# Reciprocals on a second engine, a paired fifth tile and a new order in a fused attention and feed-forward kernel

## The chip, the cores and the metric

The kernel runs on one core of one Trainium2 chip. A core has TensorE (matrix products; its weight loads are listed apart as PEld), VectorE (DVE), ScalarE (ACT), GpSimd (POOL) and SyncE (SP, which issues DMAs here). Each engine works through its own instructions in order; semaphores tie them together. The metric is device time in microseconds (us), the median of several runs. One more run was taken with the hardware profiler; its first to last instruction is called the span.

## The reference

Eight batches of eight heads, sequence 576, head size 64. Per head a linear attention with a cosine weighting, then a feed-forward layer with the activation h cos h over all 4608 tokens:

```
def phi(x, c, s):
    r = np.maximum(x, 0.0)
    return np.concatenate([r * c, r * s], axis=-1)
q_p = phi(q, cos_w, sin_w);  k_p = phi(k, cos_w, sin_w)
kv = einsum('bhsf,bhsd->bhfd', k_p, v);  z = sum(k_p, axis=2)
num = einsum('bhsf,bhfd->bhsd', q_p, kv)
den = einsum('bhsf,bhf->bhs', q_p, z)[..., None] + 1e-06
x = num / den            # (b, s) rows, 8 * 64 = 512 columns
h = x @ w_in             # 512 -> 2048
out = (h * cos(h)) @ w_out   # 2048 -> 512
```

## The kernel before

**Tiles.** A batch has 576 tokens: four tiles of 128 and a rest of 64, the fifth tile. Raw q, k and v lie in `raw[nm]`, 128 partitions by eight heads by five tile places. Batches of even and odd number use opposite halves: batch b writes five places of every second partition (`go5` in `load`, L332) and four places of the others (`go4`), so the fifth place of a batch fills only 64 partitions, and the other 64 keep what was there. Two batches' rests make one full tile of tokens: the feed-forward part runs over nine chunks of 512 tokens, eight from the full tiles of the batches and the ninth (`xR`) from the four paired fifth tiles.

**Attention.** `prep` (L355) applies relu and the cosine or sine weight (a column of `CS` per tile) to one tile, on ACT or VectorE, and writes 16-bit values to `KQ`. `cast_v` (L369) makes V 16-bit, with a column of ones, so that `kv` (L383) gives the product and the sum z in one. A tile of q is transposed by TensorE (`q_pe`, L414, batches 0 and 1) or by a transposing DMA on SP's queue (`q_dma`, L426). `num` (L435) multiplies it with `kvz`, takes the denominators (`den`, L468 and L470, eight per partition), their reciprocal (L474, VectorE) and the normalized tile (`x16`, L476, VectorE), in this order; the reciprocal and the normalization are one step of the plan, `norm`. `x_pe` or `x_dma` transposes the result to `xT`.

The fifth tile of q is scaled, transposed and kept per batch, in `qT4[0]` and `qT4[1]`. Both full-width products are added up in the PSUM bank, each batch with zero rows at the other's place; that is why the fifth place of q is set to zero at the start (L962). `late_q0` (L1039) does this for batch 0 during the first layer 1.

**Feed-forward.** `layer1` (L522) multiplies with `w_in`; `gate` (L511) takes the cosine on ACT and the product on VectorE; `layer2` (L813) multiplies with `w_out`. From chunk 3 on parts of both use a scheme with seven instead of eight products, with sums on VectorE (`sums`, L321).

**Order.** The code adds steps to a `Plan` (L142). `KEYS` (L17) holds a number for each step, found beforehand: its place in the overall order, and in the last digit which of the allowed engines takes it (`pick`, L186). `run` sorts by these places and issues; nothing is decided on the chip. Every engine gets its instructions in that order, DMAs included: loads and stores on SP, the weights' loads on POOL. Some small POOL casts (`hold_raw`, L945, and the `hold` functions in L920 to L958) write one element of a buffer only to make a following load wait until the time is right.

Of the kernel before, what the change touches and what calls it, by code (L numbers as in the profile page):

```python
# [11 lines left out]
ALU = mybir.AluOpType  # L12
F32 = mybir.dt.float32
# [180 lines left out]
def kernel(  # L194
# [9 lines left out]
    nc = tc.nc  # L204
    B, H, S, D = q.shape
    Dm, Dff = moe_w_in.shape
    P = 128
# [886 lines left out]
```

## Time and profile before

| what | value |
|---|---|
| runs | 280.79 us median of 3 (280.42 to 281.32) |
| the profiled execution | 280.85 us, span 279.0 us |
| busy | TensorE 269.2, VectorE 251.4, ACT 218.9, GpSimd 8.3 us |
| reciprocals (L474) | 36, 197 ns each |
| normalizations (L476) | 32 of 512 columns at 692 ns, 8 half ones at 421 and 414 ns |
| transposing DMAs of q (L428) | 30 |
| first matmul of layer 1 | 20.44 us from the span's start |

How to read it: the groups of a profile page name line, engine, operation, what is written from what, shape and count, then the busy time and the mean duration of one in ns, then the idle time of the engine just before them and what ended it. In the timeline the first column is the start in us, the second the duration. A releaser is written behind an arrow. The time of the run is larger than the span by what lies around it (1.85 us here).

### The profile page before, as it was taken

The numbers are of one execution on the slowest core, as the hardware profiler recorded it, in microseconds if no ns is written. First come the engines' busy times: TensorE is split into PE (matmuls) and PEld (weight loads), VectorE is DVE, ScalarE is ACT, GpSimd is POOL, SyncE is SP. The second block draws the span as 40 slices with busy tenths as digits, with TensorE's granted clock in tenths as the row PEclk, the third lists the DMA queues.
The fourth block names the chain that finished last, engine by engine and source line by source line (L and its number), as shares of the span: only waits on it lengthen the run. The fifth ranks groups of instructions, "written<-read, shape, count | busy, mean of one in ns | idle before, by whom it ended". The sixth has DMA issues, their size and how long they took to land.

```text
span 279.0 us, 6853 instructions
## 1 busy us (share of the span) xinstructions
PE 269.2 (96%) x2715; PEld 217.3 (78%) x2715; DVE 251.4 (90%) x449; ACT 218.9 (78%) x401; POOL 8.3 (3%) x21
## 2 busy tenths in 40 slices
PE   7779999999999999999999999999999999999994
PEld 2458767678766677789879887998788888888883
DVE  2977798999999999999999999999999999998872
ACT  2856698899999999999999999984684686777210
POOL 1430020000000000000000000000000000000000
PEclk9999999999999999999999999999999999999999
DMA  6999999999999999999999999737210400200324
GB/s 208 315 201 232 281 312 282 309 218 172 328 269 253 210 288 247 310 235 230 245 264 195 346 277 265 154 58 205 39 39 4 188 2 0 78 0 2 151 78 150
DMA packets 77599, 53.30 MB, mean 191 GB/s; under 512 B 46080, under 2 KB 75264, under 8 KB 77568
## 3 DMA queue, kind: packets, MB, share of 16 engines
q1 hardware_dynamic: 72608, 48.12, 67.7%
q0 software_dynamic: 4224, 4.19, 9.3%
q10 hardware_dynamic: 736, 0.57, 0.6%
q8 instruction: 21, 0.34, 0.5%
q14 instruction: 10, 0.08, 0.1%
HBM read 36.74 MB, written 9.44 MB: 166 GB/s over the span
## 4 chain that ended last, share of the span: by engine, by line
PE 85%; DMA 5%; ACT 4%; DVE 3%; issue 2%; ACTq 0%
PE M L849 33%; PE M L685 15%; PE M L542 8%; PE M L582 7%; PE TR L685 6%; PE M L784 4%; PE ATT L450 3%; DMA qT<-KQ 3%; PE ATT L391 3%; DMA qm<-in_q_dram 2%; ACT KQ L364 2%; PE TR L582 1%; ACT ch L514 1%; PE M L420 1%; DVE KQ L365 1%
## 5 line engine op out<-in xcount | busy, mean ns | idle before, releaser
L514 ACT ACTIVATE ch<-M 128x512 f32<-128x512 f32 x90 | 53.9, 603 | 14.0 <-PE M L685 6.8
L849 PEld LDWEIGHTS <-gT 128*128 128x128 f16 x560 | 54.1, 98 | 8.2
L519 DVE TENSOR_TENSOR gT<-M,ch 128x512 f16<-128x512 f32 x84 | 55.9, 685 | 4.5 <-ACT ch L514 4.0
L849 PE MATMUL M<-w_out_sb,gT 128*128 128x256 f16 x448 | 56.4, 273 | 0.0
L364 ACT ACTIVATE KQ<-km,CS 128x512 f16<-128x512 f32 x56 | 38.9, 732 | 0.5 <-DMA km<-in_k_dram 0.5
L364 ACT ACTIVATE KQ<-qm,CS 128x512 f16<-128x512 f32 x48 | 33.5, 728 | 4.4 <-DMA qm<-in_q_dram 4.2
L685 PEld LDWEIGHTS <-w_in_sb 128*128 128x128 f16 x320 | 31.0, 98 | 4.6 <-issue 0.2
L849 PE MATMUL M<-T,S 128*128 128x256 f16 x256 | 31.5, 273 | 0.0
L318 ACT ACTIVATE ost<-M 128x512 f32<-128x512 f32 x32 | 19.2, 600 | 15.0 <-PE M L849 9.5
L542 PE MATMUL M<-xT,w_in_sb 128*128 128x256 f16 x256 | 30.1, 272 | 0.6 <-DVE gT L519 0.5
L542 PEld LDWEIGHTS <-w_in_sb 128*128 128x128 f16 x256 | 24.6, 98 | 4.8 <-issue 1.2
L582 PE MATMUL M<-xT,w_in_sb 128*128 128x512 f16 x112 | 27.9, 379 | 0.0
L849 PEld LDWEIGHTS <-S 128*128 128x128 f16 x256 | 24.9, 98 | 3.4
L476 DVE TENSOR_TENSOR x<-ATT,rec 128x512 f16<-128x512 f32 x32 | 22.1, 692 | 2.5
L685 PEld LDWEIGHTS <-WS 128*128 128x128 f16 x216 | 20.6, 98 | 2.6
L582 PEld LDWEIGHTS <-w_in_sb 128*128 128x128 f16 x128 | 11.9, 98 | 9.2
L365 DVE TENSOR_SCALAR KQ<-qm,CS 128x512 f16<-128x512 f32 x32 | 14.2, 479 | 4.8 <-DMA qm<-in_q_dram 4.8
L450 PEld LDWEIGHTS <-qT 128*128 128x128 f16 x320 | 14.7, 98 | 4.4 <-issue 1.4
L323 DVE TENSOR_TENSOR S<-gT 128x2048 f16<-128x2048 f16 (+1 forms) x16 | 17.2, 1083 | 0.0
L450 PE MATMUL ATT<-kvz,qT 128*128 128x65 f16 x288 | 15.3, 194 | 0.9 <-DVE kvz L406 0.4
L323 DVE TENSOR_TENSOR gT<-Z,ch 128x1024 f16<-128x1024 f32 x13 | 15.9, 1219 | 0.3
L698 DVE TENSOR_TENSOR Z<-M,Z 128x512 f32<-128x512 f32 x22 | 14.9, 686 | 0.9 <-PE M L685 0.5
(138 smaller groups left out, 448.6 us busy)
## 6 DMA issues: line engine op xcount, KB each, us to landing
out_dram<-ost SPq DMA_DIRECT2D x33, 256.0 KB, 2.7
qm<-in_q_dram SPq DMA_DIRECT2D x8, 640.0 KB, 5.7
km<-in_k_dram SPq DMA_DIRECT2D x8, 640.0 KB, 6.5
qm<-in_q_dram SPq DMA_DIRECT2D x8, 512.0 KB, 6.0
km<-in_k_dram SPq DMA_DIRECT2D x8, 512.0 KB, 6.5
vm<-in_v_dram SPq DMA_DIRECT2D x6, 640.0 KB, 6.8
vm<-in_v_dram SPq DMA_DIRECT2D x6, 512.0 KB, 6.6
w_in_sb<-in_moe_w_in_dram POOLq DMA_DIRECT2D x4, 512.0 KB, 8.6
```

The source lines that it names most:

```text
L318: "ACT": lambda: nc.scalar.activation(out=out_, in_=in_, func=AF.Copy),
L323: return lambda: q.tensor_tensor(out=out_, in0=in0, in1=in1, op=op)
L364: fn = {"ACT": lambda: nc.scalar.activation(out=out_, in_=in_, func=AF.Relu, scale=sc), "DVE": lambda: nc.vector.tensor_scalar(out=out_, i ...
L365: "DVE": lambda: nc.vector.tensor_scalar(out=out_, in0=in_, scalar1=0.0, scalar2=sc, op0=ALU.max, op1=ALU.mult)}
L450: nc.tensor.matmul(bank[hb][:, hh * D1:(hh + 1) * D1], lhsT=a[:, h, :], rhs=z[:, h, :], start=(i == 0), stop=(i == len(parts) - 1))
L476: nc.vector.tensor_tensor(out=split(x16[n][:, hs, :], k), in0=A[:, :, :, 0:D], in1=split(rec[n][:, hs], k).unsqueeze(3).broadcast_to((P, k ...
L514: act(0.5, due, lambda: nc.scalar.activation(out=ch[c], in_=bank, func=AF.Sin, bias=math.pi / 2.0, scale=1.0), [key], [("ch", c)])
L519: dve(0.61, due, lambda: nc.vector.tensor_tensor(out=dst, in0=a, in1=b, op=ALU.mult), [key, ("ch", c), *rd], dkeys)
L542: nc.tensor.matmul(M1[m][:, jj * 2 * P:(jj + 1) * 2 * P], lhsT=w_in_sb[:, cc, j * P:(j + 1) * P], rhs=X[:, cc, ts], start=(jj == 0 and cc ...
L582: nc.tensor.matmul(M, lhsT=w_in_sb[:, cc, j * P:(j + 1) * P], rhs=X[:, cc, :], start=(cc == 0), stop=(cc == NCT - 1))
L685: nc.tensor.matmul(bank[0][:, j * TH:(j + 1) * TH], lhsT=a(cc, j), rhs=b[:, cc, :], start=(first and j == 0 and cc == 0), stop=(last and j ...
L849: nc.tensor.matmul(bank[0][:, tt * MH:(tt + 1) * MH], lhsT=a[:, j, tt * P:(tt + 1) * P], rhs=b[:, j, :], start=(first and (apart or tt == ...
```

## The change

1. The reciprocal becomes a step of its own. On VectorE it is the same instruction; on GpSimd it is a power: `den` to the power of `NEG8`, a new tile of eight values of minus one. 23 of the 36 go to GpSimd, two of them in the first attention (tiles 0 and 2 of batch 0) and 21 in batches 2 to 7.
2. The fifth tile of q is scaled and transposed once per pair of batches, at the odd one, over all 128 partitions; a new column of `CS` holds its weights for both. There is one `qT4`. Its product takes 64 columns of `qT4` (every second) for each batch and writes them to 64 neighbouring partitions, so the rows of that tile are in another order, which the last stores undo. `late_q0` and the zeroing of q go.
3. All places in `KEYS` are new, and so is the choice of engine for some steps: of q's and k's scalings, V's casts (two of batch 1 go to GpSimd) and copies from PSUM. In the first attention, the load of the third quarter of `w_in` now stands behind the first power on POOL.

```diff
-    cs_np = np.zeros((P, 2, 2, NT + 1), dtype=np.float32)
+    cs_np = np.zeros((P, 2, 2, NT + 2), dtype=np.float32)
...
+            cs_np[n::2, :, g, NT + 1] = w[NT:S5:NT + 1, None]
...
+    NEG8 = sb("NEG8", [P, 8], F32)
...
-    qT4 = [sb(f"qT4_{n}", [P, H, P]) for n in range(2)]
+    qT4 = sb("qT4", [P, H, P])
...
-        sc = CS[:, b % 2, g, t:t + 1]
+        sc = CS[:, b % 2, g, t + (nm == "q" and t == NT):][:, 0:1]
...
-                for i, (a, z) in enumerate(parts):
+                for n2 in range(2) if t == NT else [None]:
+                    rows_, cols, z = (slice(0, P), slice(0, P), kvz[b % 2]) if n2 is None else (
+                        slice(n2 * R, (n2 + 1) * R), slice(n2, P, 2), kvz[n2])
                     nc.tensor.matmul(
-                        bank[hb][:, hh * D1:(hh + 1) * D1], lhsT=a[:, h, :], rhs=z[:, h, :],
-                        start=(i == 0), stop=(i == len(parts) - 1))
+                        bank[hb][rows_, hh * D1:(hh + 1) * D1], lhsT=a[:, h, cols], rhs=z[:, h, :],
+                        start=True, stop=True)
...
+        either(due, {"DVE": 0.14, "POOL": 0.3}, {
+            "DVE": lambda: nc.vector.reciprocal(out=rec[n], in_=den[n]),
+            "POOL": lambda: nc.gpsimd.tensor_tensor(out=rec[n], in0=den[n], in1=NEG8, op=ALU.pow)},
+            [("den", n, h) for h in range(H)], [("rec", n)], port=False, hint=2)
+
         def norm():
-            nc.vector.reciprocal(out=rec[n], in_=den[n])
             for A, (hs, k, ks) in zip(N, cut):
...
-            put(due, dst.rearrange("i (p t) m -> p t i m", t=NT + 1)[:, NT], blocks(O, n)[:, i0:, f],
+            put(due, dst.rearrange("i (p t) m -> p t i m", t=NT + 1)[:, NT], O[n * R:(n + 1) * R, i0:, f],
...
-        for i, nm in enumerate("qkv"):
+        for i, nm in enumerate("kv"):
             dve(0.53, i - 9, lambda nm=nm: nc.vector.memset(raw[nm][:, :, NT, :], 0.0), [],
...
-        for t in range(NT + 1):
+        for t in range(NT + b % 2):
...
-    late_q0()
```

More of the change, by code (lines that the diff above doesn't have):

```diff
@@ L226 @@
             w = fn(theta)
-            cs_np[n::2, n, g, :] = w[:S5].reshape(R, NT + 1)
+            cs_np[n::2, n, g, :NT + 1] = w[:S5].reshape(R, NT + 1)
+            cs_np[n::2, :, g, NT + 1] = w[NT:S5:NT + 1, None]
             cs_np[1 - n::2, n, g, :NT] = w[S5:].reshape(R, NT)
@@ L237, in sb @@
         return pool.tile(shape, dt, name=name)
-    CS = sb("CS", [P, 2, 2, NT + 1], F32)
+    NEG8 = sb("NEG8", [P, 8], F32)
+    CS = sb("CS", [P, 2, 2, NT + 2], F32)
     IDENT = sb("IDENT", [P, P])
@@ L411, in qdst @@
     def qdst(b, t):
-        return (qT[t], ("qT", t)) if t < NT else (qT4[b % 2], ("qT4", b % 2))
+        return (qT[t], ("qT", t)) if t < NT else (qT4, "qT4")
     def q_pe(b, t, bank, key, eng, due):
@@ L439, in num @@
         keys = [p[1] for p in pair] if pair else [("ATT", 0), ("ATT", 1)]
-        parts = [(qdst(b, t)[0], kvz[b % 2])]
+        a = qdst(b, t)[0]
         rd = [qdst(b, t)[1]] + [("kvz", b % 2, i) for i in range(2)]
         if t == NT:
-            parts.insert(0, (qT4[1 - b % 2], kvz[1 - b % 2]))
-            rd += [("qT4", 1 - b % 2)] + [("kvz", 1 - b % 2, i) for i in range(2)]
+            rd += [("kvz", 1 - b % 2, i) for i in range(2)]
         def mm(hb):
@@ L448, in mm @@
                 h = hb * HB + hh
-                for i, (a, z) in enumerate(parts):
+                for n2 in range(2) if t == NT else [None]:
+                    rows_, cols, z = (slice(0, P), slice(0, P), kvz[b % 2]) if n2 is None else (
+                        slice(n2 * R, (n2 + 1) * R), slice(n2, P, 2), kvz[n2])
                     nc.tensor.matmul(
-                        bank[hb][:, hh * D1:(hh + 1) * D1], lhsT=a[:, h, :], rhs=z[:, h, :],
-                        start=(i == 0), stop=(i == len(parts) - 1))
+                        bank[hb][rows_, hh * D1:(hh + 1) * D1], lhsT=a[:, h, cols], rhs=z[:, h, :],
+                        start=True, stop=True)
         full.update((key, False) for key in keys)
         for hb in range(2):
-            pe(HB * len(parts), MMA, due, lambda hb=hb: mm(hb), rd, [keys[hb]])
+            pe(HB * (1 + (t == NT)), MMA, due, lambda hb=hb: mm(hb), rd, [keys[hb]])
         if pair is None:
@@ L479, in norm @@
                     op=ALU.mult)
-        dve(0.9 if pair is None else 1.02, due, norm, keys + [("den", n, h) for h in range(H)], [("x16", n)])
+        dve(0.7 if pair is None else 0.82, due, norm, keys + [("rec", n)], [("x16", n)])
         return n
@@ L767, in store_tile @@
             dst = out.rearrange("(i n s) m -> n i s m", n=2, s=S)[n][2 + i, 0:S5, 0:MH]
-            put(due, dst.rearrange("(p t) m -> p t m", t=NT + 1)[:, NT], blocks(ost[o], n)[:, i, 0:MH],
+            put(due, dst.rearrange("(p t) m -> p t m", t=NT + 1)[:, NT], ost[o][n * R:(n + 1) * R, i, 0:MH],
                 [("ost", o, 0, i)], *((nc.scalar, "ACT") if n else (nc.sync, "SP")), nb=65.5)
@@ L908, in setup @@
         nc.gpsimd.memset(V1[:, :, :, D], 1.0)
+        nc.gpsimd.memset(NEG8, -1.0)
     wi = moe_w_in.rearrange("(c p) f -> p c f", p=P)
@@ L1037, in attention @@
                 x_dma(b, t, n, due + 1)
-    def late_q0():
-        for g in range(2):
-            prep(0, "q", NT, g, "DVE", 24, after=[("g", 0, 0, 0)])
-        q_pe(0, NT, TR, ("TR", 0), "ACT", 25)
     first_attention()
     layer1(0)
-    late_q0()
     second_attention()
```

244 rows, old and new, of the table KEYS are left out of this document.

## The prediction

> **What bounds the kernel now.** I read the page's busy times and its chain that ended last, then the busy times by stage.
>
> ```profile
> PE 269.2 (96%) x2715; PEld 217.3 (78%) x2715; DVE 251.4 (90%) x449; ACT 218.9 (78%) x401; POOL 8.3 (3%) x21
> PE 85%; DMA 5%; ACT 4%; DVE 3%; issue 2%; ACTq 0%
> ```
> ```profile
> 20.00:40.00 20.00, 19.34 (x164) 15.04 (x162) 16.24 (x32) 14.84 (x26) 1.66 (x3) 1.00 1.15 277
> 40.00:80.00 40.00, 39.90 (x449) 29.86 (x448) 38.14 (x83) 37.20 (x76) 0.00 (x0) 1.00 1.05 267
> 80.00:134.00 54.00, 53.56 (x585) 42.40 (x583) 51.97 (x91) 52.90 (x102) 0.00 (x0) 1.00 1.11 247
> 134.00:188.00 54.00, 53.93 (x581) 45.28 (x580) 52.61 (x92) 52.19 (x95) 0.00 (x0) 1.00 1.01 228
> 188.00:242.00 54.00, 54.00 (x497) 46.80 (x495) 52.46 (x83) 34.95 (x61) 0.00 (x0) 1.00 0.23 70
> ```
> The columns are stretch, length, then PE, PEld, DVE, ACT and POOL busy. TensorE is the bound from 20 us on, at full clock. A busy matmul may still wait, so I also compared the distance of neighbouring matmul starts in the trace with their usual pace (109 ns for 256 columns, 216 for 512, 30 for 65, 56 for a transpose). What exceeds the pace adds up to 3.35 us after 20 us: 1.36 in 20 to 40, 1.99 later. So VectorE, though busy 97% in the middle, costs TensorE little there, and freeing it can win 2 us at most. Time lost before the first layer-1 matmul (20.44) is paid nearly in full, and that stage is a chain of single steps. From the timeline, start and duration:
>
> ```profile
> 11.09 3.34 POOL L928 DMA_DIRECT2D w_in_sb<-in_moe_w_in_dram  x4 [0.30 <-POOL w_in_sb L922]
> 17.55 1.48 POOL L942 DMA_DIRECT2D w_out_sb<-in_moe_w_out_dram  x2 [0.30 <-POOL w_out_sb L932]
> ...
> 17.44 0.20 DVE L474 RECIPROCAL rec<-den 128x8 f32<-128x8 f32 x1 [0.59 <-ACT den L468]
> 17.75 0.69 DVE L476 TENSOR_TENSOR x<-ATT,rec 128x512 f16<-128x512 f32 x1
> 18.36 0.19 DVE L474 RECIPROCAL rec<-den 128x8 f32<-128x8 f32 x1
> 18.65 0.76 DVE L476 TENSOR_TENSOR x<-M,rec 128x256 f16<-128x256 f32 x2
> ...
> 20.44 0.81 PE L542 MATMUL M<-xT,w_in_sb 128*128 128x256 f16 x6
> ```
> The last normalization that layer 1 waits for ends at 19.41; the first matmul follows 1.03 later (transpose, copy). GpSimd has only these loads and small casts to do.
>
> **The change, part by part.** The sum is made against the profiled execution, 280.85 us (span 279.0), 0.06 above the median of 280.79.
>
> *The paired fifth tile.* The pass for batch 0 (eight transposes in 20 to 40 us) goes: 8 x 56 ns of TensorE, -0.45. Eight scalings go (0.72 us on ACT, 0.48 on VectorE), one copy of 1.01 on ACT and three transposing DMAs; these lie beside TensorE and cost nothing now. The DMAs do hold SP's queue (1.63 us each, median) and so the transposes behind them; what that gives TensorE is in the stall term below. The memset of q (0.48 us, done at 1.42) gates the second load of q, but that starts at 1.54 because SP's first issue lasts to 1.48: nothing. The product of the fifth tile keeps 16 matmuls of 65 columns; its weights are now 64 columns at stride two. If none of these loads overlapped it would cost 64 x (98 - 30 ns) = 4.3 us; in the trace all weight loads of this line overlap, so 0. The last stores read 64 neighbouring partitions instead of every second one, with the same bytes; the spread of their landings (1.85 to 2.18 us) bounds it by 0.3 either way; I take 0.
>
> *The reciprocals, by VectorE's account.* Start to start, a reciprocal costs 0.31 us (17.44 to 17.75): 23 x 0.3 = 6.9 us off VectorE. By the bound above, this alone gives TensorE nothing certain. With the new order I take half of the later stalls, -1.0 (bounds 0 and -2.0; a worse order could also add as much).
>
> *The reciprocals, on GpSimd.* No row shows a power. Below it lies the small GpSimd cast (0.17 us), above it twice the longest software routine in the GpSimd rows, a DMA issue of 0.94 (a logarithm and an exponential), 1.9. A power is a routine and no single operation, so I take the mean DMA issue, 0.84, plus 0.06 until another engine sees it (POOL to PE in the trace). VectorE works in order, so everything behind a normalization waits with it. In the new written order, 21 of the 23 lie in the steady part: three normalizations have nothing between the power and themselves (0.90 each), six have one step (0.39 to 1.13 long, 1.9 together), the rest two or more and no wait at 0.84. That is 4.6 us of waiting against 6.3 freed: no loss in all, but local ones; I take +0.4 (bounds 0 and 4.6).
>
> *The start.* Powers of tiles 0 and 2 of batch 0 stand in the start. In the built program one more POOL instruction stands directly ahead of the first power: it reloads the library of GpSimd code that holds the operation. Before has none. It stands behind three w_in loads, so it begins near 11.09 + 3 x 0.84 = 13.6. Its nearest rows: the table load of ACT, and loads that engines ask for in these stretches.
>
> ```profile
> L907 ACT ACT_TABLE_LOAD x1 | 1.3, 1283 | 1.6 <-PEq L1078 1.6
> ```
> ```profile
> w_in_sb<-in_moe_w_in_dram POOLq DMA_DIRECT2D x4, 512.0 KB, 8.6
> vm<-in_v_dram SPq DMA_DIRECT2D x4, 320.0 KB, 8.3
> vm<-in_v_dram SPq DMA_DIRECT2D x4, 256.0 KB, 8.2
> ```
> The last column is us to landing. Ends: 1.3, and 12.7 for the slowest w_in load (5.9 the fastest). Code must be fetched through the same busy DMA engines, and at 256 to 512 KB the size hardly matters, so I take 8.2. Then the power starts at 21.8 and the normalization of tile 0 at 21.8 + 0.84 + 0.06 = 22.7; with 0.69 and the 1.03 to the first matmul this is 24.4, against 20.44: +4.0 (bounds 0 and 8.5). Queued behind that power on POOL: the third-quarter w_in load, the four marks that let SP load batch 1, and w_out's first half. The w_in part is needed only half of layer 1 later (7 us of matmuls), and batch 1 by as much later as layer 1 is; TensorE's 1.36 us of stalls in 20 to 40 absorb some: -0.3 (0 to -1.36).
>
> The Trainium skill speaks against this change here: its GPSIMD Engine Reference (2.1, Instruction dispatch) says that the first call into freshly loaded GpSimd code pays about 6 us (5.95 measured), with no profile instruction to show it. No run here shows it yet. By that estimate the start would cost about 1.7 instead of 4.0 and the sum would be 281.2, as in rival C below.
>
> GpSimd also takes two casts of V of batch 1 (0.28 us on VectorE, 0.41 on ACT each); its queue is empty there and other casts are written beside them: 0.
>
> Sum: -0.45 - 1.0 + 0.4 + 4.0 - 0.3 = +2.65, so 283.5 us.
>
> **Rivals.**
> A. *The reload hides* (faster). It needs no operand, so it runs while POOL would idle: the den of tile 0 comes at about 17.4, which is 3.8 us after 13.6. Up to that length it costs nothing; for it speaks ACT's 1.3 us. Then 280.85 - 0.45 - 1.0 + 0.1 = 279.5. It decides below a reload of 5.5 us, where the sum is zero.
> B. *The power is long.* At 1.6 us the three bare normalizations wait 1.66 each, the six 6.3 together, five with two steps 2.8: 14.1 against 6.3 freed, 7.8 net. VectorE's idle time from 40 to 242 us is 6.8 (stage table), so TensorE loses 1.0 to 7.8, say 4.4 in place of 0.4, and the start 0.8 more: 288.3. GpSimd's low share of work speaks for no queueing; that a power is software speaks for the length.
> C. *The reload takes the fastest fetch,* 5.9 us: first matmul at 22.1, +1.7 at the start, +0.35 in all, 281.2: no change. This is also where the skill's figure points.
> D. *The order or the stride-two weights lose:* up to +4.3 without any reload, 283 to 285. All weight loads of that line overlap today, which speaks against it.
>
> **How the numbers follow.** Forecast (reload 6.5 to 10, power up to 1.2) 0.38, own range 281.8 to 285.5; A 0.18; B 0.28; C 0.10; D 0.06. The time is the forecast's, 283.5. The range reaches down to A less some stalls, 279.3, and up to B with half a microsecond more, 288.9; outside remain long reload and long power together, and a cleaner order. 0.3% (0.84 us) is about what this measurement can tell from no change. Faster: A and a little of C, 0.20. Same: most of C, 0.10. Slower: 0.70.
>
> **What would show it.** Right: the first L542 matmul near 24.4; GpSimd silent from about 13.6 until a power ends near 22.6; the w_in load behind it issued after that; normalizations with gaps put down to POOL; TensorE stalls from 40 us on of about 1 to 1.5 us; VectorE near 245 us busy. Wrong: first matmul by 21 (A); powers of 1.5 us or more and TensorE gaps spread over 60 to 210 us (B); long weight loads in the fifth tile's product (D).

## The result and the profile after

The changed kernel takes 289.02 us (median of 4, 288.82 to 289.18) against 281.06 us of the kernel before on the same chip (280.42 to 281.52): ratio 1.0285, 95% interval 1.0261 to 1.0308. It is slower by 8 us. The forecast was 283.5 with a range of 279.3 to 288.9; the measured time lies 0.1 us above its upper end. The profiled execution has a span of 287.1 us, 8.1 more than before. Line numbers are those of the changed kernel: `den` L473 and L475, reciprocal L479 (VectorE) and L480 (GpSimd), normalization L485, product of q L455, layer 1 L551 and L694, layer 2 L858, sums L327.

Busy times and the chain that ended last, from the page:

```profile
PE 269.9 (94%) x2707; PEld 216.4 (75%) x2707; DVE 244.8 (85%) x423; ACT 216.2 (75%) x392; POOL 54.3 (19%) x47
PE 51%; issue 16%; POOL 10%; ACT 8%; DVE 6%; DMA 6%; SPq 1%; POOLq 0%; ACTq 0%; DVEq 0%
```

VectorE was relieved as forecast: 244.8 us against 251.4. GpSimd did 46 us more, and it now holds 10% of the chain; before, it was not on the chain at all. TensorE's busy time is about the same, and its share of the chain fell from 85% to 51%. The stage table (stretch, length, then PE, PEld, DVE, ACT and POOL busy, granted clock, DMA share, GB/s) says where:

```profile
20.00:40.00 20.00, 18.42 (x154) 14.48 (x152) 15.32 (x30) 13.29 (x23) 5.27 (x6) 1.00 1.11 266
40.00:80.00 40.00, 38.68 (x442) 29.06 (x441) 36.31 (x81) 35.52 (x68) 2.60 (x3) 1.00 1.03 267
80.00:134.00 54.00, 52.37 (x555) 39.91 (x554) 49.76 (x84) 51.96 (x97) 14.29 (x8) 1.00 1.03 241
134.00:188.00 54.00, 51.48 (x542) 42.34 (x540) 48.62 (x77) 48.62 (x89) 18.66 (x9) 1.00 1.01 219
188.00:242.00 54.00, 53.55 (x508) 46.06 (x506) 49.73 (x78) 34.97 (x65) 6.30 (x3) 1.00 0.22 62
```

TensorE ran at full clock in all these stages, and lost time in every one of them. Counted as in the prediction, by starts that lag behind the usual pace, its stalls after 20 us are 11.65 us against 3.35: 8.3 more. From the first matmul of layer 1 to the last matmul, what is left without the stalls fell by 1.3 us (251.05 to 249.75; more on this under the pairing), and the stretch behind the last matmul grew by 0.8 (4.33 to 5.17). Together this is 7.8 of the 8.1 us. The largest stalls lie at 60 to 80 (1.51), 107 to 134 (2.29), 134 to 161 (2.26) and 161 to 188 us (1.58), mostly at L455. Three groups (the first is the normalization in the kernel before) and four waits (engine and line, what it waited for, us in all, times, longest; the last is of the kernel before) give the chain:

```profile
L476 DVE TENSOR_TENSOR x<-ATT,rec 128x512 f16<-128x512 f32 x32 | 22.1, 692 | 2.5
L480 POOL TENSOR_TENSOR rec<-den,NEG 128x8 f32<-128x8 f32 x23 | 44.2, 1924 | 137.9 <-ACT den L473 107.3
L485 DVE TENSOR_TENSOR x<-ATT,rec 128x512 f16<-128x512 f32 x32 | 22.0, 687 | 11.9 <-POOL rec L480 11.2
```
```profile
DVE x L485 <- POOL rec L480: 11.2, 12, 1.5
...
PEld L455 <- issue: 7.8, 13, 1.4
...
PE ATT L455 <- DVE x L485: 4.9, 8, 1.3
```
```profile
PEld L450 <- issue: 1.4, 4, 0.5
```

A power takes 1.92 us in the mean, where 0.84 was taken. VectorE stands at 12 normalizations for it, 11.2 us together. The next product of q writes the PSUM bank that the normalization still has to read, so TensorE waits there. Idle time ahead of the weight loads of the same line, which the profile gives to nothing, is 7.8 us; before it was 1.4.

The start, on GpSimd and TensorE (timeline: start, duration, idle time before and its releaser in brackets):

```profile
10.83 2.97 POOL L938 DMA_DIRECT2D w_in_sb<-in_moe_w_in_dram  x3 [0.31 <-POOL w_in_sb L932]
16.84 1.67 POOL L480 TENSOR_TENSOR rec<-den,NEG 128x8 f32<-128x8 f32 x1 [3.04 <-DVE den L475]
...
20.21 1.66 POOL L480 TENSOR_TENSOR rec<-den,NEG 128x8 f32<-128x8 f32 x1 [0.26 <-DVE den L475]
```
```profile
20.48 1.03 PE L551 MATMUL M<-xT,w_in_sb 128*128 128x256 f16 x8
...
22.65 0.40 PE L505 MATMUL TR<-IDENT,x 128*128 128x128 f16 x4 [0.92 <-DVE x L485]
22.88 2.35 PE L551 MATMUL M<-xT,w_in_sb 128*128 128x256 f16 x20
```

The first power starts 0.09 us after its denominator (16.58 + 0.17). Whatever the reload of GpSimd's library ahead of it takes, it was over by then: at most the 3.04 us between the third load of `w_in` and the power. Whether the code was already in place, the runs do not tell. The first layer-1 matmul starts at 20.48, as before (20.44), and not at 24.4. What the start loses is the second power's wait, 0.92 us at the transpose of tile 2.

Last, why the mean is 1.92. From VectorE's and GpSimd's timelines:

```profile
123.03 0.15 DVE L475 TENSOR_SCALAR den<-ATT 128x8 f32<-128x8 f32 x1
123.11 1.21 DVE L327 TENSOR_TENSOR S<-gT 128x2048 f16<-128x2048 f16 x1
124.24 0.48 DVE L369 TENSOR_SCALAR KQ<-qm,CS 128x512 f16<-128x512 f32 x1
125.85 0.69 DVE L485 TENSOR_TENSOR x<-ATT,rec 128x512 f16<-128x512 f32 x1 [1.14 <-POOL rec L480]
```
```profile
123.33 2.49 POOL L480 TENSOR_TENSOR rec<-den,NEG 128x8 f32<-128x8 f32 x1 [3.46 <-DVE den L475]
...
140.37 1.64 POOL L480 TENSOR_TENSOR rec<-den,NEG 128x8 f32<-128x8 f32 x1 [2.36 <-ACT den L473]
```

The power at 123.33 begins while a sum with two inputs in SBUF runs (to 124.32), and lasts 0.85 us longer than the one at 140.37, about what the sum still had to go (0.99). The new order put two VectorE steps, 1.69 us by their durations, between denominator and normalization, and still VectorE stood 1.14 us.

### The profile page after: what moved, and what is told of

It is laid out like the page before. It is cut to its first block, busy times and chain, and to the rows that moved or that the text cites. A ratio compares the mean times of both kernels' runs of the same rounds, so it can differ in the third digit from the quotient of the medians.

```text
span 287.1 us, 6835 instructions
## 1 busy us (share of the span) xinstructions
PE 269.9 (94%) x2707; PEld 216.4 (75%) x2707; DVE 244.8 (85%) x423; ACT 216.2 (75%) x392; POOL 54.3 (19%) x47
## 4 chain that ended last, share of the span: by engine, by line
PE 51%; issue 16%; POOL 10%; ACT 8%; DVE 6%; DMA 6%; SPq 1%; POOLq 0%; ACTq 0%; DVEq 0%
PE M L858 25%; PE M L694 12%; POOL rec L480 9%; PE TR L694 5%; PE M L591 3%; DMA vm<-in_v_dram 3%; ACT KQ L368 3%; DMA km<-in_k_dram 3%; ACT ch L523 3%; PE M L551 2%; DVE x L485 2%; PE ATT L455 2%; PE ATT L395 2%; DVE gT L528 1%; POOL w_in_sb L938 1%
## 5 line engine op out<-in xcount | busy, mean ns | idle before, releaser
L480 POOL TENSOR_TENSOR rec<-den,NEG 128x8 f32<-128x8 f32 x23 | 44.2, 1924 | 137.9 <-ACT den L473 107.3
L523 ACT ACTIVATE ch<-M 128x512 f32<-128x512 f32 x90 | 52.2, 597 | 13.3 <-PE M L694 6.6
L858 PEld LDWEIGHTS <-gT 128*128 128x128 f16 x560 | 54.3, 98 | 7.7
L858 PE MATMUL M<-w_out_sb,gT 128*128 128x256 f16 x448 | 56.6, 273 | 0.0
L694 PEld LDWEIGHTS <-w_in_sb 128*128 128x128 f16 x320 | 30.8, 98 | 5.5 <-issue 1.2
L368 ACT ACTIVATE KQ<-km,CS 128x512 f16<-128x512 f32 x49 | 33.8, 719 | 0.1
L368 ACT ACTIVATE KQ<-qm,CS 128x512 f16<-128x512 f32 x43 | 30.2, 721 | 4.3 <-DMA qm<-in_q_dram 4.3
L858 PE MATMUL M<-T,S 128*128 128x256 f16 x256 | 32.4, 273 | 0.0
L485 DVE TENSOR_TENSOR x<-ATT,rec 128x512 f16<-128x512 f32 x32 | 22.0, 687 | 11.9 <-POOL rec L480 11.2
L322 ACT ACTIVATE ost<-M 128x512 f32<-128x512 f32 x34 | 20.1, 598 | 14.5 <-PE M L858 9.4
L551 PE MATMUL M<-xT,w_in_sb 128*128 128x256 f16 x256 | 29.9, 273 | 0.7 <-DVE gT L528 0.5
L551 PEld LDWEIGHTS <-w_in_sb 128*128 128x128 f16 x256 | 24.8, 98 | 4.7 <-issue 1.1
L858 PEld LDWEIGHTS <-S 128*128 128x128 f16 x256 | 24.6, 98 | 3.5
L694 PEld LDWEIGHTS <-WS 128*128 128x128 f16 x216 | 20.7, 98 | 3.4 <-issue 0.2
L455 PEld LDWEIGHTS <-qT 128*128 128x128 f16 (+1 forms) x320 | 13.9, 100 | 9.6 <-issue 7.8
L716 ACT ACTIVATE ch<-Z 128x1024 f32<-128x1024 f32 x14 | 14.8, 1057 | 7.5 <-DVE Z L707 7.5
L455 PE MATMUL ATT<-kvz,qT 128*128 128x65 f16 (+1 forms) x288 | 14.5, 194 | 5.0 <-DVE x L485 4.9
L369 DVE TENSOR_SCALAR KQ<-qm,CS 128x512 f16<-128x512 f32 x29 | 13.2, 482 | 5.1 <-DMA qm<-in_q_dram 5.1
L327 DVE TENSOR_TENSOR S<-gT 128x2048 f16<-128x2048 f16 (+1 forms) x16 | 17.3, 1080 | 0.0
```

The lines of the kernel that those rows point to most:

```text
L322: "ACT": lambda: nc.scalar.activation(out=out_, in_=in_, func=AF.Copy),
L327: return lambda: q.tensor_tensor(out=out_, in0=in0, in1=in1, op=op)
L368: fn = {"ACT": lambda: nc.scalar.activation(out=out_, in_=in_, func=AF.Relu, scale=sc), "DVE": lambda: nc.vector.tensor_scalar(out=out_, i ...
L455: nc.tensor.matmul(bank[hb][rows_, hh * D1:(hh + 1) * D1], lhsT=a[:, h, cols], rhs=z[:, h, :], start=True, stop=True)
L480: "POOL": lambda: nc.gpsimd.tensor_tensor(out=rec[n], in0=den[n], in1=NEG8, op=ALU.pow)},
L485: nc.vector.tensor_tensor(out=split(x16[n][:, hs, :], k), in0=A[:, :, :, 0:D], in1=split(rec[n][:, hs], k).unsqueeze(3).broadcast_to((P, k ...
```

## The experiments

Three theories were set against each other. **T1**: the length of the power, which the normalization behind it waits for. **T2**: the new order and the pairing lose by themselves. **T3**: handing work to GpSimd, or the port it shares with VectorE, costs something whatever operation runs there. The kernel before was run beside each: 280.64 us median with the first four kernels, 280.58 with the second four, 280.83 with the last two.

### All reciprocals back on VectorE

The last digit of a step's number in `KEYS` picks its engine; it goes from 2 to 1 for the 23 reciprocals, in the same places. Batch 3, tile 0, as an example:

```diff
-    83362,
+    83361,
```

> The changed kernel with all 36 reciprocals on VectorE, at the same places of the same order; pairing and order stay. Theory 1 (the length of the power is the whole loss: powers of 1.64 to 2.75 us, 11.2 us of waiting in front of the normalizations): the stalls of TensorE after 20 us fall from 11.65 us to about the 3.35 of before or less, the time to 279.5 to 280.5 us. Theory 2 (the new order or the paired fifth tile loses by itself, and the powers only show it): the time stays above 284 us.

Measured: 282.45 us (280.01 to 283.76), ratio 1.0042 (1.0008 to 1.0075). 6.6 of the 8 us go with the powers, so T1 holds for most. It is not faster than before, though: order and pairing bring nothing, and by the median they lose a little. The twelve runs are wide apart: four lie at 280.0 to 280.5 us, no slower than the kernel before, the others at 281.4 to 283.8. That remainder is taken up below.

### A multiplication in the power's place

```diff
-            "POOL": lambda: nc.gpsimd.tensor_tensor(out=rec[n], in0=den[n], in1=NEG8, op=ALU.pow)},
+            "POOL": lambda: nc.gpsimd.tensor_tensor(out=rec[n], in0=den[n], in1=NEG8, op=ALU.mult)},
...
-        nc.gpsimd.memset(NEG8, -1.0)
+        nc.gpsimd.memset(NEG8, 0.0)
```

> The changed kernel with a multiplication by zero in place of the power on GpSimd: same engine, same operands, same semaphores and places (the normalized tiles are zero, so attention is left out of the result). Theory 1 (length): if a multiplication takes 0.2 to 0.4 us on GpSimd, the waits in front of the normalizations nearly vanish and the time is that of the kernel with the reciprocals on VectorE, within 0.5 us, 279 to 280.5. Theory 3 (the hand-over to GpSimd and the SBUF port that it shares with VectorE cost, whatever runs there): more than half of the 8 us stays, 285 us or more.

Measured: 282.04 us (280.95 to 284.05), ratio 1.0055 (1.0026 to 1.0084). The same 23 steps on GpSimd, from the groups of this kernel:

```profile
L480 POOL TENSOR_TENSOR rec<-den,NEG 128x8 f32<-128x8 f32 x23 | 10.2, 445 | 162.1 <-ACT den L473 126.1 <-DVE den L475 36.1
```

0.45 us each instead of 1.92, and the list of VectorE's waits names GpSimd no more. The hand-over over two engines is harmless; T3 falls as the cause of the 8 us. Single multiplications took up to 1.17 us where the median is 0.20, so the shared port is seen here too, but costs nothing at this length.

### Only the start's two on VectorE

```diff
-    17012,
+    17011,
...
-    19672,
+    19671,
```

> The changed kernel with the two powers of the first attention back on VectorE, 21 powers stay. The first matmul of layer 1 is at 20.48 in the changed kernel and 20.44 before, so theory 1 puts the loss in the steady part: 287 to 288.2 us, a gain of 0.8 to 2. Had the start been the cause, as predicted, some 4 us would come back: 285.

Measured: 288.08 us (287.94 to 288.86), ratio 1.0273 (1.0247 to 1.0298). The start is worth 0.94 us, the 21 powers of the steady part 5.6 (288.08 less 282.45). In the traces 0.6 of the 0.94 are stalls, and the first matmul of layer 1 comes 0.35 earlier (20.12). That second part is not shown to be the powers': four other kernels of these experiments with the same steps up to there (both reciprocals on VectorE) have their first matmul anywhere from 19.84 to 20.52.

### The prices alone

A kernel without attention and feed-forward: powers one after another, then a power beside two equal VectorE instructions of three kinds.

```
power(SRC)                       # the first power of the program
for n in (8, 8, 4, 16, 32): power(SRC, n)
...
nc.vector.tensor_tensor(out=big[2], in0=big[0], in1=big[1], op=ALU.subtract)   # two in SBUF
nc.vector.tensor_tensor(out=f16, in0=ps, in1=f32, op=ALU.mult)                 # PSUM and SBUF
nc.vector.tensor_scalar(out=f16, in0=f32, scalar1=0.0, scalar2=SRC[:, 0:1], op0=ALU.max, op1=ALU.mult)
```

> No attention at all: prices by themselves. It runs powers alone on GpSimd (the first of the program, then 4, 8, 16 and 32 values per partition), a multiplication, and powers beside VectorE instructions that start just ahead: a sum with two SBUF inputs, a product of PSUM and SBUF, a scaling of SBUF to 16 bit. Theory: the first power starts without a gap of several us (no reload to be seen), or the gap shows the reload; 8 values take 1.64 us alone and the time grows with the number of values (0.2 us each by 1.64 / 8); beside the two-input sum the power lasts until the sum is over plus 1.64, beside the product of PSUM and SBUF 1.64. If the excess of the long powers is not the shared port, all kinds show the same length.

Measured, from its groups with the shapes kept apart, and from its timeline:

```profile
L41 POOL TENSOR_TENSOR s<-SRC,NEG 128x32 f32<-128x32 f32 x1 | 5.4, 5426 | 0.0
L41 POOL TENSOR_TENSOR s<-SRC,NEG 128x16 f32<-128x16 f32 x1 | 2.9, 2899 | 0.0
...
L41 POOL TENSOR_TENSOR s<-SRC,NEG 128x4 f32<-128x4 f32 x1 | 1.0, 1007 | 0.0
```
```profile
0.79 0.12 POOL L46 MEMSET SRC<- 128x32 f32 x1
0.99 15.99 POOL L41 TENSOR_TENSOR s<-SRC,NEG 128x8 f32<-128x8 f32 x9
...
17.10 2.48 DVE L68 TENSOR_TENSOR big<-big,big 128x2048 f16<-128x2048 f16 x2
17.27 2.54 POOL L41 TENSOR_TENSOR s<-s,NEG 128x8 f32<-128x8 f32 x1 [0.28 <-DVE s L63]
...
22.92 1.64 POOL L41 TENSOR_TENSOR s<-s,NEG 128x8 f32<-128x8 f32 x1 [0.28 <-DVE s L63]
...
26.76 1.80 POOL L41 TENSOR_TENSOR s<-s,NEG 128x8 f32<-128x8 f32 x1 [0.28 <-DVE s L63]
...
30.89 0.20 DVE L81 RECIPROCAL s<-s 128x8 f32<-128x8 f32 x1
```

A power of eight columns takes 1.64 us, eight times VectorE's reciprocal (0.20). It grows with the columns: 1.01, 2.90 and 5.43 us for 4, 16 and 32, so 0.16 us a column and 0.4 on top. Beside the two sums it takes 2.54, beside PSUM products 1.64, beside scalings 1.80. The sums are no longer than usual: two take 2.48 us together, 1.22 and 1.23 with the gap between them left out, and one took 1.22 in the kernel before (mean). And the first power of the program starts 0.08 us after the memset before it, though in the built program the reload stands between them: nothing of it is to be seen on the engine.

### The pairing alone

The kernel before in its own order, with only the paired fifth tile (`qT4`, the new column of `CS`, 64-column products, no `late_q0`).

> The kernel before, in its own order, with one part of the change alone: the fifth tiles of q go to TensorE in pairs (late_q0), so 8 transposing matmuls of 0.056 us fewer; all 36 reciprocals stay on VectorE where they were. The three V casts stay where they were. It tells what of the remaining 1.8 us of rec_dve (282.45 against 280.64) is the pairing. If the pairing does what its price says: 0.45 us less than before, 280.2 us, ratio 0.997 to 0.999. If the paired weights or the later start of the second batch's first product cost something (rival D of the prediction): 281 to 282.5, a ratio over 1.001, and then the order need not be blamed.

Measured: 280.78 us (280.65 to 282.45), ratio 1.0016 (0.9995 to 1.0037). What the pairing saves does not come back as time, and nothing over 0.4% is lost. It saves more than the transposes. In the trace of before, sixteen products of the fifth tile in a row take 0.65 us, here 0.45: a load of 64 columns is longer (110 ns median, 98 before), but the two 64-column products of a pair, which go to opposite halves of the partitions, start together, mostly within 5 ns, so the products follow one another every 17 ns in the mean instead of 32. From the first matmul of layer 1 to the last, TensorE's time without stalls is 249.91 us against 251.05: 1.1 less, of which 0.45 are the transposes. Half of it goes in stalls (3.76 against 3.19 in the same stretch). The rest is outweighed in this execution, at 281.3 us one of the longer ones, by a first matmul at 21.21 instead of 20.44 and 0.3 us more behind the last. As starts spread by 0.7 us between kernels that are alike up to there (19.84 to 20.52, above), this trace does not show that the pairing causes either.

### Six powers where they are covered

```diff
-    83362,
+    83361,
...
```

This is the edit for 17 of the 23. The powers of batch and tile (3,4), (4,0), (5,2), (6,3), (7,1) and (7,4) stay.

> The changed kernel with 17 of its 23 powers put back on VectorE; powers stay on GpSimd in the six places where VectorE has at least about 2.5 us of other work between the denominator and the normalization. T1 (a power costs only what of its 1.6 to 2.7 us the normalization behind it waits for): these six cost nothing, the time is that of rec_dve, 282.4 us or up to 0.5 less since VectorE is spared 6 x 0.2 us; ratio 1.000 to 1.006. T3 (each power costs its share wherever it stands): 6 of 23 of the loss of 6.6 us, 1.7 us over rec_dve, 284.1, ratio about 1.012.

Measured: 282.44 us (281.15 to 284.84), ratio 1.0055 (1.0026 to 1.0083): the time of the kernel without any power. From its groups:

```profile
L473 POOL TENSOR_TENSOR rec<-den,NEG 128x8 f32<-128x8 f32 x6 | 12.7, 2124 | 157.0 <-ACT den L466 118.2 <-DVE den L468 38.8
```

These six are longer than the mean (2.12 us), and no wait of VectorE names them. A power with enough VectorE work behind its denominator costs nothing that can be told from zero here (the interval is 0.8 us to either side), as T1 says; but it also gains nothing.

### The powers in the order of before

```diff
-            nc.vector.reciprocal(out=rec[n], in_=den[n])
+            if (b, t) in POWS:
+                nc.gpsimd.tensor_tensor(out=rec[n], in0=den[n], in1=NEG8, op=ALU.pow)
+            else:
+                nc.vector.reciprocal(out=rec[n], in_=den[n])
```

> The kernel before in its own order, unpaired, with the same 23 reciprocals made as powers on GpSimd and the normalization left where it stood, right behind. It tells whether the new order is part of the loss or a part of the remedy. T1: VectorE waits at nearly every one of the 23 for the power's 1.64 us and the hand-over, less what lies between them; the loss is larger than the changed kernel's 8 us: 290 to 293 us, ratio 1.032 to 1.045, so the new order had bought back a part. T2 (the order and the pairing lose by themselves, the powers little): less than the changed kernel's loss, 284 to 287 us.

Measured: 294.37 us (293.82 to 294.81), ratio 1.0484 (1.0454 to 1.0513), a little above what T1 gave. VectorE's wait, from the list of waits:

```profile
DVE x L482 <- POOL rec L478: 19.4, 16, 2.3
```

In the old order the 23 powers cost 13.8 us (294.37 less 280.58), in the new one 6.6. So the new order is a remedy for the powers: it hides about half of them. T2 falls as the main cause; what the order loses by itself is the 1.8 us above.

### Every power twice

```diff
-            "POOL": lambda: nc.gpsimd.tensor_tensor(out=rec[n], in0=den[n], in1=NEG8, op=ALU.pow)},
+            "POOL": lambda: (nc.gpsimd.tensor_tensor(out=TWO, in0=den[n], in1=NEG8, op=ALU.pow),
+                nc.gpsimd.tensor_tensor(out=rec[n], in0=den[n], in1=NEG8, op=ALU.pow))},
```

> The changed kernel with every one of the 23 powers done twice in a row on GpSimd (the first into a scratch tile), the rest as it is: the length goes from 1.64 to 3.3 us, or to 4.3 beside a sum, and nothing else changes. T1: every further us is waited for by the normalization where the cover is used up already; 23 x 1.64 = 37.7 us are added, of which TensorE's queue ahead of it hid 60% of the first dose and hides less of the second: 18 to 30 us more than the changed kernel, 307 to 319 us. T2 or T3 (order, or the hand-over as such): the time stays within 3 us of 289.

Measured: 320.4 us (two runs, 318.63 and 322.18), ratio 1.1412 (1.1345 to 1.1478). Groups and a wait:

```profile
L481 POOL TENSOR_TENSOR TWO<-den,NEG 128x8 f32<-128x8 f32 x23 | 43.8, 1906 | 131.7 <-ACT den L474 104.3 <-DVE den L476 27.1 <-DVE rec L480 0.3
L481 POOL TENSOR_TENSOR rec<-den,NEG 128x8 f32<-128x8 f32 x23 | 40.0, 1737 | 0.0
```
```profile
DVE x L486 <- POOL rec L481: 39.5, 20, 3.1
```

The first 44.2 us of powers cost 6.6 us; the next 40.0 cost 31.4, a little over the expected 18 to 30. What cover there is goes with the first dose, and after that nearly every microsecond is paid. T2, and T3 as a price of the hand-over alone, would have left the time near 289.

### What remains: one cast of the new order

The kernel without powers was still 1.8 us above before. Its trace, of an execution of 282.81 us, shows two places that the kernel before doesn't have. One is on ScalarE and then on TensorE:

```profile
129.66 0.72 ACT L361 ACTIVATE KQ<-km,CS 128x512 f16<-128x512 f32 x1 [1.27 <-DMA km<-in_k_dram]
130.29 0.58 ACT L516 ACTIVATE ch<-M 128x512 f32<-128x512 f32 x1
```
```profile
131.64 0.60 PE L687 MATMUL M<-XS,w_in_sb 128*128 128x256 f16 x4 [0.83 <-DVE gT L521]
```

A cast of the next batch's k stands in ScalarE's queue before its load has landed; the gate behind it comes late, and TensorE stalls about 1.0 us. The kernels with six powers and with multiplications show the same 1.3 to 1.4 us wait. In the changed kernel itself the wait is not there; that the powers had delayed everything else is the likely reason, but not shown. The other place is larger, 1.7 us at 154 to 156 us, where the product of q waits for a transposing DMA:

```profile
PE ATT L448 <- DMA qT<-KQ: 1.6, 1, 1.6
```

Two transposing DMAs ahead of it occupied SP's queue for 2.48 and 2.04 us; with six powers, in the same order, these took 1.39 and 1.49, and neither that kernel nor the one with multiplications has a wait there. It belongs to the execution, then, and not to the order alone. With both places gone the stalls of this trace, 6.04 us, would be 3.3, as before.

The cast was tested. The step was moved behind the gate, the gated copy and a denominator, once in the kernel without powers and once in that with six:

```diff
-    128972,
+    131072,
```

> rec_dve (the changed kernel with all 36 reciprocals on VectorE) with one step of the new order moved: ScalarE's cast of the seventh batch's k, tile 3, cosine half, goes behind the gate, the gated copy and the denominator that it stood ahead of. In rec_dve's trace ScalarE waited 1.27 us there for the load of k (128.39 to 129.66 us), the gate behind it came late, and TensorE's layer-1 matmul stood idle for about 1.05 us; six_pow and the kernel with multiplications show the same 1.07 and 1.21 us, the kernel before shows nothing there. If this misplaced cast is what the new order loses by itself: 1.0 us less than rec_dve's 282.45, 281.4 us, ratio to before 1.000 to 1.003. If the order's loss lies elsewhere or is spread: 282.3 us or more, ratio 1.004 to 1.007, and what remains stays open.

> The kernel with six powers (six_pow) with the same one step moved, as a second reading of the same question: 281.4 us against its 282.44 if the misplaced cast is the order's loss, ratio to before 1.000 to 1.004; 282.3 or more, ratio 1.005 to 1.008, if not.

Measured: 281.68 us (279.89 to 283.23), ratio 1.0028 (1.0001 to 1.0055), and 281.32 us (280.42 to 283.75), ratio 1.0018 (0.9993 to 1.0043). In both traces the wait is gone and TensorE's stalls of 107 to 134 us are 0.3 instead of 1.28 and 1.07. The median times fell by 0.8 and 1.1 us, in the expected direction and size, but the intervals of the pairs overlap; the traces show the mechanism more clearly than the times its price. They are also of short executions, 280.00 and 280.42 us, with spans of 278.2 and 278.6, below the 279.0 of before; the late DMA is missing there too, and the first of them starts layer 1 at 19.84 instead of 20.50, so the 2.8 us between the spans without powers (281.0 and 278.2) are not the cast's alone. The first lies between what was expected of the misplaced cast (281.4) and of a loss elsewhere (282.3), the second is at 281.4 within 0.1. What is left in the medians, 0.5 to 0.9 us over before, is not in these two executions at all, so their traces cannot say where it lies. The late DMA is a candidate that no run tests, and the rest stays open. No kernel here beats the one before by its median.

## Why the prediction was wrong, step by step

**The power's length.** This is the step that failed: "I take the mean DMA issue, 0.84", within bounds of 0.17 and 1.9. It is 1.64 us alone and 1.92 in the mean. The nearest row was chosen by kind (a software routine), and the size of the work wasn't asked for: the price goes by columns. With it fell the next term, "+0.4 (bounds 0 and 4.6)" for VectorE's waits: measured 5.6 us. The upper bound was worked out with 0.84 and not with the 1.9 that stood above it, so it was no bound.

**The two-input sums.** The prediction had no term for a power that lasts longer beside VectorE's sums. That is the difference of 1.64 and 1.92, up to 2.75 in a single case, and it also spoils the cover: a sum between denominator and normalization hides little, because the power waits for its end first. The Trainium skill has the rule: its page SBUF — State Buffer (Who interferes with whom) says that a VectorE instruction with two SBUF inputs contends with a GpSimd instruction that reads SBUF. The prices agree: 2.54 beside such sums, 1.64 beside products that read PSUM. The same section says of VectorE's two-port modes that whoever issues first gets the shared pair for the whole instruction. For a sum and a power the runs show only half of that: the power lasts longer by most of what the running sum has left, but the second sum, which started while the power ran, was not held up (1.23 us after 1.22).

**The library's reload.** Taken at 8.2 us, +4.0 at the start; it costs nothing that can be seen. The first power starts 0.09 us after its denominator, 3.04 us after GpSimd's last work. Here rival A was right, with a first matmul at 20.48. The figure of about 6 us in the Trainium skill's GPSIMD Engine Reference (2.1, Instruction dispatch) would have ended the reload at 13.80 + 5.95 = 19.75; the power starts at 16.84, so the measurement speaks against it for this operation, if the reload stands behind the loads as the prediction has it.

**The second power of the start.** Not a term of the forecast. B's 0.8 us was something else, the greater length of the first power ahead of layer 1, and that did not show: the first matmul came in time. What the start lost, 0.94, is near it by chance.

**The new order.** "I take half of the later stalls, -1.0" did not come. Without powers the new order has its own wait of 1.3 us on ScalarE, and freed time of VectorE is worth little to TensorE: the kernel with multiplications takes the 23 reciprocals off VectorE without making it wait, and is 0.4 us faster than the one with all of them on VectorE, within the intervals. What the order does is hide powers, 7.2 us of them.

**The pairing.** -0.45 in the forecast; the work is gone (2707 matmuls instead of 2715, and 1.1 us of TensorE in all), the time isn't. The prediction took the fifth tile's product as unchanged. Its 64-column weight loads are longer, as rival D feared (110 ns median against 98), but the product is shorter all the same.

**The sum.** The start was put at +3.7 (4.0 less 0.3) and is +0.94: 2.8 too much. The steady powers were put at +0.4 and are +5.6: 5.2 too little. Order and pairing were put at -1.45 and are +1.8 (282.45 against 280.64): 3.3 too little. Together 5.7 us, from +2.65 to +8.4 (289.02 less the 280.64 measured beside the first experiments), so the start's error hid part of the others. That the measured time missed the range by only 0.1 us owes something to this. Rival B named what happened: a power of 1.6 us, VectorE's waits, gaps spread over 60 to 210 us, 288.3. It had a chance of 0.28, on the ground that a power is software. Of its 14.1 us of waits, 11.2 came, and TensorE lost 5.6 in the steady part against its 4.4. But its 288.3 also held the forecast's +3.7 for the reload, with 0.8 on top, where 0.94 came, and the -1.45 for order and pairing, where +1.8 came. These two errors, 3.6 too much and 3.3 too little, cancel: the mechanism was right, the closeness of the time is luck.

## What to carry to other kernels

Work moved from a busy engine to an idle one leaves the busy engine's queue but not the chain of dependences: if the next step of the old engine needs the result, it waits for the new engine's price, and here that was 1.9 us in place of 0.2. Ask first whether the relieved engine held up the bound at all (3.35 us of stalls was the most there was to win), then measure the operation by itself at its real size. When the price is unknown, carry its upper bound through every term that hangs on it.

## What the runs showed that was not expected

- The power on GpSimd costs by the columns of a partition: 1.01, 1.64, 2.90 and 5.43 us for 4, 8, 16 and 32 columns; a multiplication of eight takes 0.20.
- A power that starts while VectorE runs a sum of two SBUF inputs lasts longer by roughly what the sum has left (2.54 instead of 1.64 beside sums of 1.22 us); a scaling from SBUF to SBUF of 0.48 us gives 1.80, a product with one input in PSUM nothing. A running power lengthened no sum: both sums that followed each other beside it took 2.48 us together.
- Two products whose weights have 64 columns each and which write opposite halves of the partitions start together, mostly within 5 ns: one follows another every 17 ns in the mean, where products with full weights follow every 32, although the 64-column load is longer (110 ns against 98).
- The load of GpSimd's library before the first power left no gap: 0.09 us behind its denominator in the changed kernel, 0.08 us behind the memset in the kernel of prices.
